# An RWKV kernel with a dense SiLU block: r and k transposed in two row groups behind the previous unit's A product, one ring of five PSUM banks, two units reordered

## Chip, cores, metric

One core of one Trainium2 chip. Times are microseconds (us) of device time for the whole program, medians over several executions. TensorE is the matmul engine, VectorE, ScalarE and GpSimd the three others; PSUM is the matmul output memory in eight banks, SBUF the working memory.

## The reference

```python
# r, k, v: (B=4, H=8, S=768, D=48); w, u: (H, D)
for t in range(S):
    cur = einsum('bhd,bhe->bhde', u[None] * kt, vt)
    y[:, :, t] = einsum('bhd,bhde->bhe', rt, state + cur)
    state = w[None, :, :, None] * state + einsum('bhd,bhe->bhde', kt, vt)
x = y.transpose(0, 2, 1, 3).reshape(B * S, H * D)      # 3072 x 384
h = x @ w_in                                           # 384 -> 2048
return (h * sigmoid(h)) @ w_out                        # 2048 -> 384
```

The kernel cuts time into six chunks of 128 tokens. A *unit* is one chunk of one batch entry: 24 units, unit i = (chunk i // 4, batch i % 4). Inside a unit the recurrence becomes matmuls: r and k are turned (tokens to columns) and multiplied by powers of w; A = kT x rT is masked; y = A x v + r x state; the unit's sum of k x v updates the state.

## The kernel before

The parts that the change touches (cuts marked with `# ...`):

```python
def p1(i, tag="tA", mid=None, spins=0):        # turn r and k, apply the decays
    tr = ps.tile([128, NP, C], FP, name="tr", tag=tag, bufs=3)
    tk = ps.tile([128, NP, C], FP, name="tk", tag=tag, bufs=3)
    spin(spins, tr)                            # keep-warm matmuls
    for t, src in ((tr, rin), (tk, kin)):
        flat = src[n].rearrange("p h d -> p (h d)")
        for p in range(NP):                    # NP = 4 pairs of heads
            nc.tensor.transpose(t[0:PR, p, :], flat[:, 128 * p:128 * p + PR], ident)
    L["rT"] = wrk.tile([PR, NP, C], FP, name="rT")
    nc.vector.tensor_tensor(out=L["rT"], in0=tr[0:PR], in1=lamR, op=ALU.mult)
    # ... kT the same from tk and lamK; if i >= B: ScalarE converts rT to rT16

def p2(i, spins=0):                            # the A product, even and odd heads
    ae = ps.tile([128, NP, C], FP, name="ae", tag="tA", bufs=3)
    ao = ps.tile([128, NP, C], FP, name="ao", tag="tA", bufs=3)
    for p in range(NP):
        nc.tensor.matmul(ae[:, p, :], L["kT"][0:D, p, :], L["rT"][0:D, p, :], ...)
        nc.tensor.matmul(ao[:, p, :], L["kT"][64:PR, p, :], L["rT"][64:PR, p, :], ...)
    # ... VectorE: am = a * maskM for both

for i in range(B + 2, NU):                     # units 6 to 23
    p2(i)
    fill(2)                                    # pieces of the dense block ("fillers")
    bonus_sum(i); bonus_vu(i)
    if i + 1 < NU: front(i + 1)                # p1, v16, ku, rku_f, kc of the next unit
    if i >= NIN: load(i + NIN)
    fill(1)
    p3y(i); p3e(i)                             # y = ..., y16 = y + vu
    if sc < NCH - 1: sums(i); state(i)
    fill(2)
    p4(i)                                      # turn y16
    fill(3)
    # ... refill the list of fillers with the chunk's dense products
```

`hps` is the first dense product (ScalarE takes it to `gT` through SiLU), `ops` the second; `win` and `wout` are their weights. Other names: `am` is A after its mask, `sps` the unit's sum of k x v, `st` and `stb` the state and its 16-bit copy, `xT` the turned y. GpSimd makes `kc`, the decayed k that the sum needs, and `rku_f`, the product of r, u and k; VectorE adds its rows up ("row sum", `bonus_sum`), and v times that is `vu`. Keep-warm matmuls (`spin`) multiply junk, only so that TensorE is busy. PSUM: a ring of 3 banks (tag tA), one of 2 (tag y), one of 3 (tag moe, dense).

## Time and profile before

| | before |
|---|---|
| median of the first runs | 220.91 us (220.13 to 222.15) |
| TensorE busy, of a span of 218.3 us | 205.8 us, 94% |
| saturated stage | 58 to 190 us, TensorE idle 0.2 us |
| transposes of one unit, start to start | 0.87 us |

In lines of the profile, PE is TensorE, PEld its weight loads, DVE VectorE, ACT ScalarE and POOL GpSimd; `out<-in` are tiles, L218 is a line of the kernel, x4 a count. The page's row of slices cuts the span into 40 equal parts and gives TensorE's busy share in tenths; the clock row gives the granted TensorE clock the same way:

```profile
PE   7999588878999999999999999999999999999993
PEclk9999999999999999999999999999999999999999
```

Apart from the first and the last slice, TensorE has gaps in slices 5 to 10 (22 to 55 us) only. This profiled execution had the full clock throughout.

### The profile page before, as it was taken

How to read it: one execution, taken by the hardware profiler on the slowest of the kernel's cores; microseconds unless marked ns; L12 is line 12 of the kernel's file. 1: busy time of each engine (PE TensorE's matmuls, PEld its weight loads, DVE VectorE, ACT ScalarE, POOL GpSimd, SP SyncE). 2: the span in 40 equal slices, each digit the busy share in tenths (PEclk: the TensorE clock that was granted, in tenths of full speed). 3: DMA queues.
4: the chain of work that ended last, by engine and by line, in shares of the span. 5: the costliest groups of instructions: out<-in, count | busy, mean ns of one | idle time of the engine just before them, and what ended most of it. 6: DMA issues, size and time to landing. Idle time of an engine off the chain costs nothing.

```text
span 218.3 us, 4606 instructions
## 1 busy us (share of the span) xinstructions
PE 205.8 (94%) x1778; PEld 137.1 (63%) x1778; DVE 115.0 (53%) x234; ACT 105.4 (48%) x240; POOL 113.1 (52%) x143
## 2 busy tenths in 40 slices
PE   7999588878999999999999999999999999999993
PEld 2776365557777787676567676567676557654561
DVE  6578626745384573685375476366467337420121
ACT  2487876666710563214873124782025771049400
POOL 3399774565835953848664675373475165200000
PEclk9999999999999999999999999999999999999999
DMA  4998999999534750738513465510201000110011
GB/s 95 222 223 154 199 213 188 197 212 183 114 76 104 179 114 3 159 97 175 114 36 75 110 147 116 100 39 0 75 36 38 3 0 16 60 72 0 3 72 72
DMA packets 81662, 22.32 MB, mean 102 GB/s; under 512 B 75368, under 2 KB 81256, under 8 KB 81640
## 3 DMA queue, kind: packets, MB, share of 16 engines
q1 hardware_dynamic: 78360, 18.88, 40.1%
q0 software_dynamic: 3280, 3.15, 8.7%
q8 instruction: 14, 0.23, 0.4%
q14 instruction: 8, 0.07, 0.1%
HBM read 20.45 MB, written 4.72 MB: 115 GB/s over the span
## 4 chain that ended last, share of the span: by engine, by line
PE 84%; ACT 6%; DVE 6%; issue 1%; POOL 1%; DVEq 0%; ACTq 0%
PE ops L329 29%; PE hps L317 24%; PE ae L235 11%; PE tr L218 5%; PE tk L218 3%; PE spin L123 2%; DVE rT L220 2%; PE yT L305 2%; ACT vu L206 2%; PE sps L273 2%; PE y L257 2%; ACT gT L320 1%; PE y L254 1%; PE tr L123 1%; DVE kT L224 1%; DVE am L242 1%
## 5 line engine op out<-in xcount | busy, mean ns | idle before, releaser
L317 PE MATMUL hps<-xT,win 128*128 128x512 f16 (+1 forms) x348 | 70.6, 342 | 1.6 <-ACT gT L320 0.9
L329 PE MATMUL ops<-wout,gT 128*128 128x384 f16 x384 | 69.9, 326 | 0.0
L320 ACT ACTIVATE gT<-hps 128x512 f16<-128x512 f32 (+1 forms) x116 | 58.5, 524 | 20.2 <-PE hps L317 18.2
L329 PEld LDWEIGHTS <-gT 128*128 128x128 f16 x384 | 35.8, 98 | 21.3
L198 POOL TENSOR_TENSOR vu<-vin,rku 128x384 f32<-128x384 f32 x20 | 16.6, 829 | 61.3 <-DVE rku L192 60.1
L317 PEld LDWEIGHTS <-win 128*128 128x128 f16 x348 | 32.1, 98 | 24.2 <-issue 2.6
L242 DVE TENSOR_TENSOR am<-ae,maskM 128x512 f16<-128x512 f32 x24 | 16.6, 691 | 46.1 <-PE ao L237 46.1
L227 ACT CAST rT<-rT 112x512 f16<-112x512 f32 x20 | 12.4, 618 | 50.7 <-DVE rT L220 50.7
L333 DVE COPY osb<-ops 128x384 f32<-128x384 f32 x24 | 13.3, 556 | 33.2 <-PE ops L329 32.7
L235 PEld LDWEIGHTS ae<-rT,kT 48*128 48x128 f32 x192 | 23.1, 187 | 9.1 <-issue 6.7
L235 PE MATMUL ae<-rT,kT 48*128 48x128 f32 x192 | 27.7, 285 | 0.5 <-DVE kT L224 0.2
L237 PE MATMUL ao<-rT,kT 48*128 48x128 f32 x192 | 27.7, 285 | 0.0
L175 POOL TENSOR_TENSOR ku<-kin,u_bc 128x384 f32<-128x384 f32 x24 | 24.1, 1006 | 6.4 <-ACT u_bc L145 6.4
L181 POOL TENSOR_TENSOR rku_f<-rin,ku 128x384 f32<-128x384 f32 x24 | 24.1, 1003 | 1.8
L186 POOL TENSOR_TENSOR kc<-kin,lamC 128x384 f16<-128x384 f32 x24 | 24.0, 999 | 0.0
L237 PEld LDWEIGHTS ao<-rT,kT 48*128 48x128 f32 x192 | 23.1, 187 | 0.0
L220 DVE TENSOR_TENSOR rT<-tr,pi 112x512 f32<-112x512 f32 x24 | 16.6, 690 | 10.4 <-PE tr L218 10.3
L306 ACT COPY xT<-yT 128x384 f16<-128x384 f16 x24 | 11.4, 474 | 17.0 <-PE yT L305 17.0
L242 DVE TENSOR_TENSOR am<-ao,maskM 128x512 f16<-128x512 f32 x24 | 16.3, 681 | 0.0
L224 DVE TENSOR_TENSOR kT<-tk,pi 112x512 f32<-112x512 f32 x24 | 16.3, 681 | 0.0
L291 POOL TENSOR_TENSOR sdec<-st,pi 112x384 f32<-112x384 f32 x16 | 13.3, 834 | 5.2 <-DVE st L287 5.2
L264 DVE TENSOR_TENSOR y<-y,vu 128x384 f16<-128x384 f32 x24 | 13.3, 553 | 4.0 <-PE y L257 2.7
(62 smaller groups left out, 213.9 us busy)
## 6 DMA issues: line engine op xcount, KB each, us to landing
rin<-in_r_dram SPq DMA_DIRECT2D x24, 192.0 KB, 3.4
kin<-in_k_dram SPq DMA_DIRECT2D x24, 192.0 KB, 3.4
vin<-in_v_dram SPq DMA_DIRECT2D x24, 192.0 KB, 3.5
out_dram<-osb SPq DMA_DIRECT2D x24, 192.0 KB, 1.9
wout<-in_moe_w_out_dram POOLq DMA_DIRECT2D x2, 768.0 KB, 10.6
win<-in_moe_w_in_dram POOLq DMA_DIRECT2D x2, 384.0 KB, 7.1
win<-in_moe_w_in_dram POOLq DMA_DIRECT2D x1, 768.0 KB, 11.6
wrow<-in_w_dram SPq DMA_DIRECT2D x1, 1.5 KB
```

Source lines behind the costliest of these rows:

```text
L175: nc.gpsimd.tensor_tensor(out=L["ku"], in0=kin[i % NIN][:, :, 0:D], in1=u_bc, op=ALU.mult)
L181: nc.gpsimd.tensor_tensor(out=L["rku_f"], in0=rin[i % NIN][:, :, 0:D], in1=L["ku"], op=ALU.mult)
L186: nc.gpsimd.tensor_tensor(out=kc[i % NKC][:, :, 0:D], in0=kin[n][:, :, 0:D], in1=lamC, op=ALU.mult)
L218: nc.tensor.transpose(t[0:PR, p, :], flat[:, 128 * p:128 * p + PR], ident)
L220: nc.vector.tensor_tensor(out=L["rT"], in0=tr[0:PR], in1=lamR, op=ALU.mult)
L224: nc.vector.tensor_tensor(out=L["kT"], in0=tk[0:PR], in1=lamK, op=ALU.mult)
L235: nc.tensor.matmul(ae[:, p, :], L["kT"][0:D, p, :], L["rT"][0:D, p, :], start=True, stop=True)
L237: nc.tensor.matmul(ao[:, p, :], L["kT"][64:PR, p, :], L["rT"][64:PR, p, :], start=True, stop=True)
L242: nc.vector.tensor_tensor(out=am, in0=a, in1=maskM.unsqueeze(1).broadcast_to([128, NP, C]), op=ALU.mult)
L317: nc.tensor.matmul(hps, win[:, q, ft * 128:(ft + 1) * 128], xts[sc][:, q, b0:b1, :].rearrange("p b t -> p (b t)"), start=(q == 0), stop=(q ...
L320: nc.scalar.activation(out=gts[sc][:, ft, b0 * C:b1 * C], in_=hps, func=AF.Silu)
L329: nc.tensor.matmul(ops, gts[sc][:, ft, b * C:(b + 1) * C], wout[:, ft, :], start=(ft == 0), stop=(ft == NFT - 1))
```

## The change

Its intent: fewer TensorE cycles for the f32 transposes. Those of 128 tokens by 128 columns become pairs of 64 tokens on the lower and upper half of the array's rows. They stand right behind the A product, which uses row halves too, so that they need no change of tiling mode of their own. That needs four banks at a time, hence one ring of five. Units 4 and 5 are put in a new order, with the conversion of r to 16 bit and the loading of wout later, and the state of chunk 0 read by VectorE alone.

```diff
+    def p1t(i):
+        xs = [ps.tile([128, 2, NP, 64], FP, name="xs", tag="t", bufs=5) for _ in range(2)]
+        for a, src in enumerate((rin, kin)):
+            flat = src[n].rearrange("p h d -> p (h d)")
+            for p in range(NP):
+                for g in range(2):
+                    t = slice(64 * g, 64 * g + 64)
+                    nc.tensor.transpose(xs[g][0:PR, a, p, :],
+                                        flat[t, 128 * p:128 * p + PR], ident[t, t])
+        rk = wrk.tile([PR, 2, NP, C], FP, name="rk")        # rT = rk[:, 0], kT = rk[:, 1]
+    def p1d(i):
+        for g in range(2):
+            nc.vector.tensor_tensor(out=rk[:, :, :, 64 * g:64 * g + 64], in0=xs[g][0:PR],
+                                    in1=lam(g), op=ALU.mult)
+    def r16(i): ...                                         # the 16-bit r, now on its own
-    def p2(i, spins=0):
+    def p2(i, spins=0, nxt=None):
         # ... A product; tiles now tag="t", bufs=5
+        if nxt is not None: p1t(nxt)
         # ... masks
+        if nxt is not None: p1d(nxt)
     # state, chunk 0:
-                nc.scalar.copy(out=st16[b][...], in_=sps[...])
                 nc.vector.tensor_copy(out=dst, in_=sps[p0:p0 + D, :, c0:c0 + D])
+        else:
+            nc.scalar.copy(out=st16[b], in_=st[b])
     # head:
-        p1(s, tag="moe", ..., spins=4 if s else 0)
+        p1(s, ..., spins=2 if s else 0)
-        p2(s, spins=3)
+        p2(s, spins=2)
     # ... units 4 and 5 in a new order; wout issued behind state(a), a = 4
     for i in range(B + 2, NU):
-        p2(i)
-        fill(2)
         bonus_sum(i)
         bonus_vu(i)
+        p2(i, nxt=i + 1 if i + 1 < NU else None)
+        fill(2)
         if i + 1 < NU:
             front(i + 1)                                    # no longer contains p1
+            r16(i + 1)
```

More of the change, by code (lines that the diff above doesn't have):

```diff
@@ L104 @@
     nc.gpsimd.tensor_copy(out=ident16, in_=ident)
-    pi = cst.tile([PR, 2 * NP, C + 1], FP)
+    NT = NP * (C + 1)
+    pif = cst.tile([PR, 2 * NT + 2], FP)
+    pi = pif[:, 0:2 * NT].rearrange("q (a c) -> q a c", c=C + 1)
     nc.gpsimd.memset(pi[:, :, 0:1], 1.0)
@@ L118, in spin @@
         if t is None:
-            t = ps.tile([128, 512], FP, name="spin", tag="y", bufs=2)
+            t = ps.tile([128, 512], FP, name="spin", tag="t", bufs=5)
         else:
@@ L125, in to_cols @@
     def to_cols(row):
-        t = ps.tile([128, 512], FP, name="cols", tag="y", bufs=2)
+        t = ps.tile([128, 512], FP, name="cols", tag="t", bufs=5)
         nc.tensor.transpose(t[0:PR, 0:NP], row.rearrange("p j d -> p (j d)")[:, 0:PR],
@@ L139, in to_rows @@
     def to_rows(dst, cols):
-        t = ps.tile([128, NP, 2, 64], FP, name="rows", tag="y", bufs=2)
+        t = ps.tile([128, NP, 2, 64], FP, name="rows", tag="t", bufs=5)
         for p in range(NP):
@@ L158, with lam @@
     wCT = pi[:, 0:NP, C]
+    def lam(g):
+        t = pif.rearrange("q (a n) -> q a n", a=2)[:, :, 0:NT]
+        return t.rearrange("q a (p c) -> q a p c", c=C + 1)[:, :, :, 64 * g:64 * g + 64]
     lamCT = cst.tile([PR, NP, C], FP)
@@ L207, in bonus_act, with p1 @@
                                  func=AF.Copy, scale=L["rku"][:, h:h + 1])
-    def p1(i, tag="tA", mid=None, spins=0):
+    def p1(i, mid=None, spins=0):
         n = i % NIN
         L = live.setdefault(i, {})
-        tr = ps.tile([128, NP, C], FP, name="tr", tag=tag, bufs=3)
-        tk = ps.tile([128, NP, C], FP, name="tk", tag=tag, bufs=3)
+        tr = ps.tile([128, NP, C], FP, name="tr", tag="t", bufs=5)
+        tk = ps.tile([128, NP, C], FP, name="tk", tag="t", bufs=5)
         spin(spins, tr)
@@ L218, in p1 @@
                 nc.tensor.transpose(t[0:PR, p, :], flat[:, 128 * p:128 * p + PR], ident)
-        L["rT"] = wrk.tile([PR, NP, C], FP, name="rT")
+        rk = wrk.tile([PR, 2, NP, C], FP, name="rk")
+        L["rT"] = rk[:, 0]
         nc.vector.tensor_tensor(out=L["rT"], in0=tr[0:PR], in1=lamR, op=ALU.mult)
@@ L222, in p1, with r16 @@
             mid()
-        L["kT"] = wrk.tile([PR, NP, C], FP, name="kT")
+        L["kT"] = rk[:, 1]
         nc.vector.tensor_tensor(out=L["kT"], in0=tk[0:PR], in1=lamK, op=ALU.mult)
-        if i >= B:
-            L["rT16"] = wrk.tile([PR, NP, C], F16, name="rT16")
-            nc.scalar.copy(out=L["rT16"], in_=L["rT"])
-    def p2(i, spins=0):
-        L = live[i]
-        ae = ps.tile([128, NP, C], FP, name="ae", tag="tA", bufs=3)
-        ao = ps.tile([128, NP, C], FP, name="ao", tag="tA", bufs=3)
+    def p1t(i):
+        n = i % NIN
+        L = live.setdefault(i, {})
+        xs = [ps.tile([128, 2, NP, 64], FP, name="xs", tag="t", bufs=5) for _ in range(2)]
[6 more added lines that the diff above has]
+                                        flat[t, 128 * p:128 * p + PR], ident[t, t])
+        rk = wrk.tile([PR, 2, NP, C], FP, name="rk")
+        L["rT"] = rk[:, 0]
+        L["kT"] = rk[:, 1]
+        L["xs"] = xs, rk
+    def p1d(i):
+        L = live[i]
+        xs, rk = L["xs"]
+        for g in range(2):
+            nc.vector.tensor_tensor(out=rk[:, :, :, 64 * g:64 * g + 64], in0=xs[g][0:PR],
+                                    in1=lam(g), op=ALU.mult)
+    def r16(i):
+        L = live[i]
+        L["rT16"] = wrk.tile([PR, NP, C], F16, name="rT16")
+        nc.scalar.copy(out=L["rT16"], in_=L["rT"])
+    def p2(i, spins=0, nxt=None):
+        L = live[i]
+        ae = ps.tile([128, NP, C], FP, name="ae", tag="t", bufs=5)
+        ao = ps.tile([128, NP, C], FP, name="ao", tag="t", bufs=5)
         spin(spins, ae)
@@ L238, in p2 @@
                              start=True, stop=True)
+        if nxt is not None:
+            p1t(nxt)
         L["am"] = []
@@ L245, in p2 @@
             L["am"].append(am)
+        if nxt is not None:
+            p1d(nxt)
     def p3y(i):
@@ L250, in p3y @@
         v16 = L["v16"]
-        L["y"] = y = ps.tile([128, H, D], FP, name="y", tag="y", bufs=2)
+        L["y"] = y = ps.tile([128, H, D], FP, name="y", tag="t", bufs=5)
         for p in range(NP):
@@ L268, in sums @@
         L = live[i]
-        L["sps"] = sps = ps.tile([128, NP, PW], FP, name="sps", tag="y", bufs=2)
+        L["sps"] = sps = ps.tile([128, NP, PW], FP, name="sps", tag="t", bufs=5)
         kf = kc[i % NKC].rearrange("p h d -> p (h d)")
@@ L284, in state @@
             else:
-                nc.scalar.copy(out=st16[b][p0:p0 + D, :, c0:c0 + D],
-                               in_=sps[p0:p0 + D, :, c0:c0 + D])
                 nc.vector.tensor_copy(out=dst, in_=sps[p0:p0 + D, :, c0:c0 + D])
@@ L301, in p4 @@
             xts[sc] = wrk.tile([128, NQ, B, C], F16, name="xT", bufs=3)
-        yT = ps.tile([128, NQ, C], F16, name="yT", tag="y", bufs=2)
+        yT = ps.tile([128, NQ, C], F16, name="yT", tag="t", bufs=5)
         yf = L["y16"].rearrange("p h d -> p (h d)")
@@ L363, in clear @@
         nc.scalar.copy(out=st[b], in_=zero)
-        nc.scalar.copy(out=st16[b], in_=zero)
     for s in range(B):
-        p1(s, tag="moe", mid=to_cols_u if s == 0 else None, spins=4 if s else 0)
+        p1(s, mid=to_cols_u if s == 0 else None, spins=2 if s else 0)
         nat_v(s)
@@ L403 @@
     bonus_vu(a)
-    nat_ku(b_)
-    for g in range(2):
-        nc.gpsimd.dma_start(
-            out=wout[:, 8 * g:8 * g + 8, :],
-            in_=moe_w_out[1024 * g:1024 * g + 1024, :].rearrange("(f p) n -> p f n", p=128))
-    nat_rk(b_)
     for ft in range(4):
@@ L416, in front @@
     def front(i):
-        p1(i)
         nat_v(i)
@@ L424 @@
     fillers.extend(l1s(0)[4:])
-    p1(a)
+    p1t(a)
+    p1d(a)
     fill(1)
-    nat_v(a)
     sums(0)
     state(0)
+    nat_v(a)
+    r16(a)
+    nat_kc(a)
     fill(1)
-    p2(a)
+    p2(a, nxt=b_)
     fill(1)
+    nat_ku(b_)
+    nat_rk(b_)
+    p3y(a)
+    p3e(a)
     sums(1)
@@ L435 @@
     fill(1)
-    p3y(a)
-    p3e(a)
-    nat_kc(a)
+    sums(a)
+    state(a)
+    for g in range(2):
+        nc.gpsimd.dma_start(
+            out=wout[:, 8 * g:8 * g + 8, :],
+            in_=moe_w_out[1024 * g:1024 * g + 1024, :].rearrange("(f p) n -> p f n", p=128))
+    p4(a)
+    fill(2)
+    r16(b_)
+    nat_v(b_)
+    for i in range(4):
+        load(NIN + i)
+    bonus_sum(b_)
+    bonus_vu(b_)
+    p2(b_, nxt=b_ + 1)
+    nat_kc(b_)
+    fill(2)
     sums(2)
     state(2)
-    fill(1)
-    sums(3)
-    state(3)
-    p1(b_)
-    fill(1)
-    p4(a)
-    sums(a)
-    state(a)
-    fill(1)
-    p2(b_)
-    bonus_sum(b_)
-    bonus_vu(b_)
-    nat_kc(b_)
-    fill(2)
-    nat_v(b_)
-    fill(1)
     p3y(b_)
@@ L460 @@
     state(b_)
-    for i in range(NIN):
-        load(NIN + i)
-    fill(2)
+    load(NIN + 4)
+    load(NIN + 5)
+    fill(1)
     p4(b_)
@@ L467 @@
     front(B + 2)
+    r16(B + 2)
+    sums(3)
+    state(3)
     fill(2)
@@ L470 @@
         sc, b = unit(i)
-        p2(i)
-        fill(2)
         bonus_sum(i)
         bonus_vu(i)
+        p2(i, nxt=i + 1 if i + 1 < NU else None)
+        fill(2)
         if i + 1 < NU:
             front(i + 1)
+            r16(i + 1)
         if i >= NIN:
```

## The prediction

> **What bounds the kernel now.** I read the busy times first, then the windows by stage, then the chain of waits, then single groups of instructions, then the order of time inside one unit. A unit is 128 tokens of one batch entry; there are 24 of them, numbered 0 to 23.
>
> The page and the windows (span, then busy time of TensorE, its weight loads, VectorE, ScalarE, GpSimd, clock, DMA share):
>
> ```profile
> PE 205.8 (94%) x1778; PEld 137.1 (63%) x1778; DVE 115.0 (53%) x234; ACT 105.4 (48%) x240; POOL 113.1 (52%) x143
> ...
> 0.00:30.00 30.00, 25.09 (x211) 16.73 (x212) 19.22 (x51) 19.88 (x63) 21.28 (x35) 1.00 0.98 181
> 30.00:51.00 21.00, 17.51 (x159) 11.57 (x157) 12.08 (x25) 13.90 (x33) 12.11 (x16) 1.00 1.14 196
> 51.00:58.00 7.00, 6.83 (x81) 5.99 (x79) 4.21 (x8) 4.96 (x15) 4.64 (x6) 1.00 0.97 192
> 58.00:190.00 132.00, 131.83 (x1190) 89.58 (x1188) 75.27 (x143) 56.64 (x115) 74.28 (x89) 1.00 0.34 78
> ```
>
> There are three regimes. From 58 to 190 us TensorE never stops (131.83 of 132 us) while no other engine passes 57%; there every microsecond of TensorE work removed shortens the run. From 30 to 51 us (units 4 and 5 and the states of chunk 0) TensorE is idle for 3.5 us, and it waits for VectorE, GpSimd and ScalarE in turn. Before 30 us the four first units form a chain of latencies. After 190 us only the last chunk's two dense products are left.
>
> The transposes as a group, and one unit in order of time (start, duration, engine, line):
>
> ```profile
> L218 PE MATMUL tr<-ident,rin 128*112 128x128 f32 x96 | 14.9, 279 | 0.0
> L218 PE MATMUL tk<-ident,kin 128*112 128x128 f32 x96 | 14.6, 275 | 0.0
> ...
> 70.03 0.60 PE L218 MATMUL tr<-ident,rin 128*112 128x128 f32 x4
> 70.47 0.60 PE L218 MATMUL tk<-ident,kin 128*112 128x128 f32 x4
> 70.90 0.81 PE L329 MATMUL ops<-wout,gT 128*128 128x384 f16 x4
> ```
>
> The mean of 275 ns contains latency. What one costs is the distance of starts: 70.03 to 70.90 us is 0.87 us for eight transposes, 109 ns each, with no idle. The A product of the same unit:
>
> ```profile
> 67.62 0.37 PE L235 MATMUL ae<-rT,kT 48*128 48x128 f32 x1
> 67.63 0.37 PE L237 MATMUL ao<-rT,kT 48*128 48x128 f32 x1
> 67.84 0.27 PE L235 MATMUL ae<-rT,kT 48*128 48x128 f32 x1
> 67.84 0.27 PE L237 MATMUL ao<-rT,kT 48*128 48x128 f32 x1
> 67.95 0.27 PE L235 MATMUL ae<-rT,kT 48*128 48x128 f32 x1
> ...
> 68.51 0.27 PE L237 MATMUL ao<-rT,kT 48*128 48x128 f32 x1
> 68.72 0.50 PE L329 MATMUL ops<-wout,gT 128*128 128x384 f16 x2
> ```
>
> Even and odd heads sit on rows 0 to 47 and 64 to 111; the two products start 0.01 us apart and the next pair follows after 0.11 us. So two row groups really run side by side, weight loads included. The first step is 0.21 us, not 0.11, and so is the step back to full height (68.51 to 68.72): changing between row groups and full array costs about 0.1 us on each side.
>
> **What the Trainium skill says.** "TensorE: Matmul & The Clock Gate", Part 3 on row and column tiling: matmuls in different row groups run concurrently, a few ns apart; the trace agrees (0.01 us). "TensorEngine Tiling (Array Packing)", Key Properties: changing the tiling mode drains the engine; the trace agrees (the two 0.1 us above). The same page, Gotcha 1: different row tiles may not write one PSUM bank at the same time; the change gives each row group its own bank, and no run yet shows what else would happen. "TensorE: Matmul & The Clock Gate", Back-to-back issue gap: N/2.4 GHz plus 2.5 ns. For N=384 that is 162.5 ns and the trace has 0.65 us for four ops matmuls, so 162; for the f32 transposes of 128 columns the measured 109 fits two cycles a column (107 + 2.5).
>
> **The change part by part.**
>
> 1. *Transposes in two row groups.* For 20 units (4 to 23; units 0 to 3 keep the old form) eight transposes of 128 columns become sixteen of 64 columns, in pairs on rows 0 to 63 and 64 to 127. Moving data: 64 columns at two cycles are 53 + 2.5 = 56 ns a pair if the pair is concurrent. Weight load: still 112 columns. Its latency row shows 137 ns for the transposes, 130 for the f16 load of 112 columns, 187 for the f32 load of 128 columns in the A product; the A product's load is hidden in a 110 ns period, so I estimate the transposes' load at some 50 ns net, hidden behind 56. Eight pairs: 0.45 us instead of 0.87, a saving of **0.42 us a unit**. They stand right behind the A product of the unit before, which is in row groups already, so no extra change of mode. 17 units in the saturated stage: 17 x 0.42 = **7.1 us**. The three in the stage laid out anew: 1.3 us, less 0.3 us because unit 4's stand alone and pay both mode changes: **1.0 us**.
>
> 2. *VectorE.* It still multiplies two tiles of 112x512 per unit (690 ns each), only cut by token half over r and k instead of by r and k. No gain and no loss. But the four reads (two masks, two decays) now follow each other: A end + 0.15, then 4 x 0.65 = 2.6 us until the y addition can run, and one output copy (0.56) may push in. TensorE meanwhile does 0.45 (transposes) + 3 fillers of 0.65 + 0.4 (y) + 0.2 (sums) + 2 fillers of 0.65 = 4.3 us before it needs that y. VectorE needs about 0.15 + 2.6 + 0.56 + 0.55 = 3.9 us. Slack 0.4 us: no wait expected. The row sum of unit i moves ahead of its A product, into time in which VectorE waited anyway.
>
> 3. *One ring of five banks instead of 3 + 2.* Per unit seven tiles go through five banks. At the A product four are taken (two A, two transposed); their predecessors (y, sums, y turned) have been read by then. Zero in the saturated stage. In the first four units the transposes no longer borrow the dense product's three banks, so five banks do what eight did; I count at most five tiles alive and expect no wait of size.
>
> 4. *Units 4 and 5 anew.* The state of chunk 0 today is read in four alternating steps by ScalarE and VectorE from one bank; the waits show it:
>
> ```profile
> DVE st L287 <- ACT stb L285: 3.5, 7, 1.2
> ...
> PE sps L273 <- DVE st L287: 1.3, 2, 0.7
> ...
> PE sps L273 <- POOL kc L186: 0.7, 1, 0.7
> PE hps L317 <- ACT gT L320: 0.6, 1, 0.6
> ```
>
>    After the change VectorE reads both halves in a row (0.7 us instead of 1.45) and ScalarE converts from SBUF. I followed the new order by hand with the durations above. TensorE then waits about 0.3 us before y of unit 4, 0.3 before its turning back, and **1.2 us** for GpSimd's kc of unit 5 (which comes behind the two wout issues, 0.9 us each, and vu). That is some 1.8 us where the old order loses about 4 us (3.5 in the window, a little more at its ends): **2.2 us**.
>
> 5. *Head.* Two keep-warm matmuls fewer before the transposes of units 1 to 3, at 0.216 us each; they lay between A and the next transposes, where VectorE idled 0.55, 0.12 and 0.29 us before rT. The gain is the lesser of 0.43 and that idle time each: 0.43 + 0.12 + 0.29 = **0.8 us**. Four ScalarE copies (0.5 us each) go too, but ScalarE waited there.
>
> Sum: 7.1 + 1.0 + 2.2 + 0.8 = 11.1 us off 220.9: about **210 us**. Dense products, output copies and the 20.8 us tail stay as they are.
>
> **The rivals.**
>
> *The pair doesn't run at 56 ns.* If the weight loads of f32 data bound it (112 columns at two cycles would be 93 ns, some 96 a pair), eight pairs cost 0.77 us and the change gives 2 us instead of 8: 216 us. If the two groups ran one after the other it gives nothing: 218. For: none of the rows shows a 64-column transpose. Against: the A product's loads overlap across the groups, and the load rows (137 against 187) say one cycle a column.
>
> *A new wait takes its place.* VectorE's in-order queue (mask, mask, decay, decay, output copy, y) or the row sum at the head of the loop, which waits for GpSimd's rku_f and holds back the masks. In the saturated stage GpSimd has 5.2 us of work per 7.6 us unit, so it keeps up; at unit 6, right after the new layout, it may be a microsecond late. If the y addition came 0.3 us late in every unit, 18 x 0.3 = 5.4 us would be lost: 215 us.
>
> *The late wout.* Its issue moves from 28.6 us to about 40 us, behind unit 4's state; its landing took 8.4 to 12.8 us, when DMA ran at its full 200 GB/s. It is first read at 58.2 us now and at about 54 us then. If input loads delay it, TensorE stands still for one to three us: 211 to 213 us.
>
> *The clock.* Fewer keep-warm matmuls might let the granted clock fall in the head; the gaps there are about a microsecond, the clock row is at full speed throughout, so I give this little.
>
> **Range and chances.** The 7 us of the saturated stage are the firm part, if the pairs are concurrent; the 4 us of layout and head are good to about 2 us either way. That puts 8 in 10 cases between 207 and 214 us. Faster by over 2% means below 216.5 us; it needs only half of the sum. 0.91 faster, 0.07 within 2%, 0.02 slower.
>
> **What would show it.** In the changed kernel: sixteen transposes with 64 columns, a pair every 56 ns and 0.45 us from the last A pair to the next filler's mode step; a saturated stage with TensorE over 99% and units 0.42 us shorter; waits of sums for kc of about 1 us near 42 us; first ops matmul near 54 us without a wait for DMA; states in chunk 0 without the VectorE-ScalarE alternation. The prediction is wrong if a pair takes 90 to 110 ns, if TensorE waits for y (VectorE) in every unit, or if it stands before the first ops.

## The result

The changed kernel is correct and took **210.78 us** (210.09 to 210.90, four runs) against 220.52 us for the kernel before in the same comparison. The ratio is 0.954, with a 95% interval of 0.948 to 0.960; on the chip of the first experiments it was 0.953 (0.951 to 0.954; 210.51 against 221.00 us).

The page and the windows of the changed kernel, with columns as in the prediction (the last figures are the clock, the DMA share and GB/s):

```profile
PE 197.5 (94%) x1928; PEld 129.0 (62%) x1928; DVE 115.2 (55%) x234; ACT 101.9 (49%) x232; POOL 113.7 (54%) x143
...
PEclk9999669999999999999999999999999999999999
...
0.00:30.00 30.00, 25.08 (x199) 16.21 (x200) 19.06 (x51) 18.47 (x58) 18.98 (x32) 0.89 0.97 180
30.00:54.00 24.00, 21.20 (x257) 14.82 (x256) 16.49 (x34) 16.66 (x39) 19.63 (x24) 1.00 1.10 185
54.00:182.00 128.00, 127.86 (x1350) 85.62 (x1348) 76.41 (x144) 56.73 (x120) 75.04 (x88) 1.00 0.39 88
```

TensorE's busy time fell by 8.3 us. The saturated stage is still saturated (127.86 of 128 us). The four A products of the head, from the first to the last start, took 11.41 us instead of 12.44, but unit 4's A product came at 32.41 us, as before (32.37). In between the clock was at half, from 22.7 to 29.6 us, so that it is 0.89 over the first 30 us. That fault was not in the profile of before. The longest pause of TensorE in the microseconds ahead of it (start, duration, and in brackets the idle time before and what ended it):

```profile
22.54 0.35 PE L344 MATMUL yT<-ident,y 128*128 128x128 f16 x3 [1.39 <-DVE y L303]
```

The transposes of the same kind of unit, in order of time (start and duration in us), with the step of the A product ahead and the first filler behind, and their group:

```profile
71.44 0.27 PE L272 MATMUL ao<-rk 48*128 48x128 f32 x1
71.55 0.39 PE L245 MATMUL xs<-ident,rin 64*112 64x64 f32 x8
71.78 0.39 PE L245 MATMUL xs<-ident,kin 64*112 64x64 f32 x8
72.10 0.82 PE L368 MATMUL ops<-wout,gT 128*128 128x384 f16 x4
...
L245 PE MATMUL xs<-ident,rin 64*112 64x64 f32 x160 | 7.9, 216 | 0.0
```

Sixteen transposes take from 71.55 to about 72.00 us, and the step back to full height (0.1 us, which the A product paid before) now comes behind them. Four pairs go from 71.55 to 71.78, 57 ns each. Units in the stage of ops are 7.62 us apart, from A product to A product, instead of 8.04.

What TensorE and VectorE wait for from 30 to 60 us in the changed kernel (total, times, longest):

```profile
PE sps L312 <- POOL kc L194: 1.3, 1, 1.3
PE hps L356 <- ACT gT L359: 1.1, 1, 1.1
...
DVE rku L200 <- POOL rku_f L189: 3.0, 2, 2.6
```

The first is the wait that the prediction named. The second is new; the account of it, tested in e7 below, is this: at unit 6 VectorE's queue stands at the row sum, which waits for GpSimd; masks and decays behind it come late, ScalarE's conversion of r comes late, and gT behind that.

### The profile page after: what moved, and what is told of

Read it like the earlier page. It is cut to its first block, busy times and chain, and to the rows that moved or that the text cites. A ratio compares the mean times of both kernels' runs of the same rounds, so it can differ in the third digit from the quotient of the medians.

```text
span 209.2 us, 4922 instructions
## 1 busy us (share of the span) xinstructions
PE 197.5 (94%) x1928; PEld 129.0 (62%) x1928; DVE 115.2 (55%) x234; ACT 101.9 (49%) x232; POOL 113.7 (54%) x143
## 4 chain that ended last, share of the span: by engine, by line
PE 80%; DVE 3%; POOL 3%; ACT 1%; issue 1%; ACTq 0%
PE ops L368 30%; PE hps L356 29%; PE ae L270 9%; PE xs L245 4%; PE y L296 2%; PE sps L312 2%; PE yT L344 2%; PE y L293 1%; DVE am L279 1%; POOL wout L477 1%; DVE rk L256 1%; POOL sdec L330 1%; ACT gT L359 1%; PE ao L272 1%; POOL kc L194 0%
## 5 line engine op out<-in xcount | busy, mean ns | idle before, releaser
L356 PE MATMUL hps<-xT,win 128*128 128x512 f16 (+1 forms) x348 | 71.6, 350 | 1.9 <-ACT gT L359 1.1
L368 PE MATMUL ops<-wout,gT 128*128 128x384 f16 x384 | 68.2, 326 | 0.0
L270 PEld LDWEIGHTS ae<-rk 48*128 48x128 f32 x192 | 23.1, 187 | 9.9 <-issue 6.2
L256 DVE TENSOR_TENSOR rk<-xs,pif 112x512 f32<-112x512 f32 x40 | 25.6, 681 | 5.6 <-PE xs L245 5.6
L270 PE MATMUL ae<-rk 48*128 48x128 f32 x192 | 27.7, 285 | 0.9 <-DVE rk L233 0.9
L272 PE MATMUL ao<-rk 48*128 48x128 f32 x192 | 27.7, 285 | 0.0
L326 POOL CAST stb<-st 112x384 f16<-112x384 f32 x16 | 8.1, 504 | 34.7 <-DVE st L321 34.0
L262 ACT CAST rT<-rk 112x512 f16<-112x512 f32 x20 | 12.4, 620 | 22.5 <-DVE rk L256 22.5
L272 PEld LDWEIGHTS ao<-rk 48*128 48x128 f32 x192 | 23.1, 187 | 0.0
L330 POOL TENSOR_TENSOR sdec<-st,pif 112x384 f32<-112x384 f32 x16 | 13.4, 836 | 7.2 <-DVE st L324 7.2
```

Source lines behind the costliest of these rows:

```text
L256: nc.vector.tensor_tensor(out=rk[:, :, :, 64 * g:64 * g + 64], in0=xs[g][0:PR], in1=lam(g), op=ALU.mult)
L330: nc.gpsimd.tensor_tensor(out=sdec[b], in0=st[b], in1=wCT.unsqueeze(2).broadcast_to([PR, NP, PW]), op=ALU.mult)
L356: nc.tensor.matmul(hps, win[:, q, ft * 128:(ft + 1) * 128], xts[sc][:, q, b0:b1, :].rearrange("p b t -> p (b t)"), start=(q == 0), stop=(q ...
L368: nc.tensor.matmul(ops, gts[sc][:, ft, b * C:(b + 1) * C], wout[:, ft, :], start=(ft == 0), stop=(ft == NFT - 1))
```

## The experiments

All twelve kernels gave correct results. The mean granted clock of the executions is listed, since 3.4 us at half clock lowers it by 0.008 (3.4 x 0.5 of some 209). The calls ran on three chips: the changed kernel again and e1 to e3 on one, e4 to e7 on a second, e8 to e11 on a third. Medians of different calls are compared below as they are; where a difference is small, the ratios to before, with their intervals, decide.

| kernel | median us | ratio to before | mean clock of its executions |
|---|---|---|---|
| before (call 1; calls 2 and 3) | 221.0; 220.97 and 221.0 | | 0.988 to 0.992; 0.981 to 1.0 |
| changed, again | 210.51 | 0.953 (0.951 to 0.954) | 0.984 to 0.991 |
| e1_spins | 211.38 | 0.956 (0.955 to 0.958) | 0.992 |
| e2_full_height | 216.94 | 0.981 (0.978 to 0.984) | 0.991 to 0.998 |
| e3_group_after_group | 214.56 | 0.972 (0.970 to 0.975) | 0.984 to 0.992 |
| e4_old_place | 224.03 | 1.015 (1.012 to 1.019) | 0.985 to 0.992 |
| e5_two_rings | 229.34 | 1.038 (1.034 to 1.043) | 0.985 to 0.992 |
| e6_kc_first | 209.95 | 0.951 (0.948 to 0.954) | 0.98 to 0.992 |
| e7_sum_behind_masks | 209.04 | 0.947 (0.944 to 0.950) | 0.982 to 0.992 |
| e8_old_place_late_r16 | 217.60 | 0.984 (0.981 to 0.986) | 0.984 to 0.992 |
| e9_both | 207.86 | 0.941 (0.939 to 0.944) | 0.983 to 0.992 |
| e10_both_warm | 206.74 | 0.936 (0.933 to 0.938) | 0.998 to 1.0 |
| e11_old_state | 210.58 | 0.952 (0.949 to 0.956) | 0.984 to 0.998 |

### The changed kernel again

> The changed kernel once more, unchanged, so that the experiments of this call have it on their own chip. All theories: 209.5 to 211.5 us. The trace of the changed kernel had the granted clock at half from 22.9 to 29.7 us; if that depends on chance, some executions will show a mean clock near 1.0 and be 1.5 to 2 us shorter; if it belongs to the kernel, all will show 0.98 to 0.99.

All four executions had a clock of 0.984 to 0.991; so the drop is no accident of one profile. But the seven executions of the kernel before on the same chip had 0.988 to 0.992 as well. With the later calls, before ran at 1.0 in 219.87 to 220.13 us, at 0.992 in 220.94 to 221.12 us and at 0.981 to 0.983 in 222.09 to 222.25 us. A window of 3.4 us at half clock costs about 1 us, and both kernels usually lose one. Where the kernel before loses it was not profiled; e4 and e8 below, which have its head, were at half from 38 to 41 us, between units 4 and 5. At like clock the change gains some 10.5 us.

### e1_spins: the keep-warm matmuls of the head restored

> Undoes one part: 4 and 3 keep-warm matmuls in the head again, instead of 2 and 2. Theory A (the fewer keep-warm matmuls let the clock fall): clock 1.0, the 24 half-wide hps matmuls at 26 us take 2.9 us instead of 4.7, and the time falls by 1.0 to 2.0 us against the changed kernel, less up to 0.8 us for the longer head. Theory B (the pause of TensorE from 21 to 24.5 us, while it waits for y and the masks, lets it fall; the keep-warm matmuls before 20 us are too early to matter): clock 0.98 to 0.99 again, time equal or up to 0.8 us longer.

```diff
-        p1(s, mid=to_cols_u if s == 0 else None, spins=2 if s else 0)
+        p1(s, mid=to_cols_u if s == 0 else None, spins=4 if s else 0)
-        p2(s, spins=2)
+        p2(s, spins=3)
```

0.87 us longer than the changed kernel, with the clock at 0.992 in all four executions. Theory A is out: these matmuls do not prevent the drop. And taking them out was worth about 0.9 us. Theory B's reason holds only in part: the pause behind the A product of unit 3 shrank from 1.39 us to 0.22, and the drop came all the same, at 26.8 us, behind a later pause:

```profile
22.61 0.34 PE L344 MATMUL yT<-ident,y 128*128 128x128 f16 x3 [0.22 <-DVE y L303]
...
25.79 1.82 PE L356 MATMUL hps<-xT,win 128*128 128x256 f16 x12 [1.18 <-ACT xT L345]
```

### e2_full_height: everything but the row groups

> Everything of the change but the row groups: the transposes of the next unit stand behind the A product, but as eight of full height and 128 columns. Theory (a concurrent pair takes 56 ns): 20 units lose 0.42 us each, 8.4 us, less 0.3 us for unit 4: 218 to 219.5 us, so layout, ring and head are worth some 2 us against before. Rival (the gain came from the new layout and order, the row groups only moved along): 211 to 213 us.

```diff
-                for g in range(2):
-                    t = slice(64 * g, 64 * g + 64)
-                    nc.tensor.transpose(xs[g][0:PR, a, p, :], flat[t, ...], ident[t, t])
+                nc.tensor.transpose(xs[a] ..., flat[:, 128 * p:128 * p + PR], ident)
     # p1d then multiplies xs[0] by lamR and xs[1] by lamK
```

Theory expected 218 to 219.5 us, 7.5 to 9.0 over the changed kernel; it is 6.4, below that range. The rival's 0.5 to 2.5 us are out. In order of time, from the last step of A to the filler:

```profile
71.08 0.27 PE L272 MATMUL ao<-rk 48*128 48x128 f32 x1
71.28 0.65 PE L244 MATMUL xs<-ident,rin 128*112 128x128 f32 x4
71.76 0.60 PE L244 MATMUL xs<-ident,kin 128*112 128x128 f32 x4
72.20 0.81 PE L368 MATMUL ops<-wout,gT 128*128 128x384 f16 x4
```

From the end of A (71.19 us, one step of 0.11 behind its last start) to the filler are 1.01 us; in the changed kernel 0.55 (71.55 to 72.10). The distance between units' A products says the same: 8.08 against 7.62 us. From unit 7 to unit 23 that is 129.03 against 121.69 us, so the row groups are worth 7.3 us there. But the kernel without them reached unit 7's A product at 54.01 us against 55.00: up to there they gave nothing. That stage waits for other engines, and unit 6, with its wait for gT, even took 8.95 us without them and 9.60 with them. ScalarE's conversion of r in that unit, first with the row groups (the changed kernel again), then without:

```profile
50.70 0.62 ACT L262 CAST rT<-rk 112x512 f16<-112x512 f32 x1 [1.36 <-DVE rk L256]
```

```profile
49.72 0.62 ACT L262 CAST rT<-rk 112x512 f16<-112x512 f32 x1 [0.24 <-DVE rk L256]
```

VectorE's two multiplications began at 49.34 and 49.00 us and took 1.28 us. Cut by tokens, the conversion of r starts behind the second of them; cut by r and k, behind the first, 0.69 us long. So the row groups have a cost of their own here, which e4 shows again. TensorE's wait for gT behind it was 1.1 us with them and 0.3 us without.

### e3_group_after_group: one row group after the other

> The same sixteen transposes of 64 columns in two row groups, but all eight of the first group and then all eight of the second. Theory (the gain is the two groups running side by side): each takes 56 ns alone, 0.90 us a unit instead of 0.45; 20 x 0.45 = 9 us longer, 219 to 220.5 us. Rival (the gain is that 64 columns at half height are cheaper in themselves, or TensorE overlaps the groups over a distance of eight instructions): 211 to 212.5 us.

```diff
-        for a, src in enumerate((rin, kin)):
-            for p in range(NP):
-                for g in range(2):
+        for g in range(2):
+            for a, src in enumerate((rin, kin)):
+                for p in range(NP):
```

4.1 us longer, between the two expectations. One unit in order of time (the program has r x4 and k x4 of the lower group, then r x4 and k x4 of the upper):

```profile
63.47 0.39 PE L245 MATMUL xs<-ident,rin 64*112 64x64 f32 x4
63.69 0.22 PE L245 MATMUL xs<-ident,kin 64*112 64x64 f32 x1
63.70 0.27 PE L245 MATMUL xs<-ident,rin 64*112 64x64 f32 x1
63.75 0.27 PE L245 MATMUL xs<-ident,kin 64*112 64x64 f32 x2
...
63.97 0.38 PE L245 MATMUL xs<-ident,kin 64*112 64x64 f32 x4
64.29 0.34 PE L368 MATMUL ops<-wout,gT 128*128 128x384 f16 x1
```

The upper group's first r starts 0.01 us after the lower group's first k and ahead of its second. So, by the start times of the trace, TensorE runs a matmul of a free row group ahead of some that stand before it in the program; r and k are interleaved like this in all 20 units. Part of the two groups overlaps: 0.72 us (63.47 to 64.29, less the 0.1 us of the mode step) instead of the 0.90 of no overlap and the 0.45 of pairs. The 0.27 us more than in pairs are also the difference of the units, 7.90 against 7.62 us, and 16 of them are 4.3 us. Half height with this partial overlap gives 0.18 us of a unit against e2 (8.08 to 7.90); the alternating order gives the rest.

### e4_old_place: the row groups alone, at the old place

> The row groups alone: the kernel before, with the transposes of units 4 to 23 as sixteen of 64 columns in two row groups, but at their old place between two fillers; layout, rings and head as before. Theory (a pair takes 56 ns, but here each unit pays a change of tiling mode of its own, 0.1 us before, 0.1 in the first step, 0.1 after): 0.45 + 0.3 instead of 0.87 us, 0.1 to 0.15 us a unit, 2 to 2.5 us in all: 218.5 to 219 us. Rival (the place does not matter): 17 saturated units save 0.38 us or more each, 214 to 214.7 us.

```diff
     # in the kernel before, p1 of units 4 to 23 is replaced by p1t: row groups, both
     # multiplications, then the conversion of r, all at p1's place
+        xs = [ps.tile([128, 2, NP, 64], FP, name="xs", tag="tA", bufs=3) for _ in range(2)]
```

3.1 us **slower than before** (1.2 to 1.9%); neither theory nor rival had that. In the stage of ops it does what the theory says: 7.87 instead of 8.04 us a unit. The units of hps became longer: the two with half-wide hps (6 and 9) took 9.2 instead of 8.41 us. TensorE's waits from 60 to 190 us, and ScalarE's conversion in one such unit:

```profile
PE hps L345 <- ACT gT L348: 3.3, 7, 1.1
...
81.41 1.29 DVE L252 TENSOR_TENSOR rk<-xs,pif 112x512 f32<-112x512 f32 x2 [0.33 <-PE xs L246]
...
82.78 0.62 ACT L255 CAST rT<-rk 112x512 f16<-112x512 f32 x1 [1.65 <-DVE rk L252]
```

Before, the conversion needed one multiplication (r). Cut by tokens, it needs both, 1.3 us, and ScalarE's queue stands still before it for 1.65 us with the SiLU of the next hps behind.

### e8_old_place_late_r16: the same with the conversion moved back

> The old-place kernel was 3 us slower than before, although its ops units are 0.18 us shorter (7.87 against 8.05). Here it gets one part more of the change: ScalarE converts r to 16 bit later, behind the next two fillers (in the first two units behind the fill ahead of their y). Theory (in the old place both halves of r and k must have been multiplied before the conversion can run, it blocks ScalarE's queue, gT comes late and the hps matmuls wait, 3.3 us between 60 and 190 us): those waits go, 218 to 220 us. Rival (the loss is in the mode changes or in the rings): 223 to 224.5 us again.

```diff
         fill(2)
+        if i + 1 < NU:
+            r16(i + 1)            # was inside the front of unit i + 1
         p4(i)
```

6.4 us faster than at the old place with the early conversion, 3.4 us faster than before; the waits for gT from 60 to 190 us are gone altogether. The theory holds, though the time lies 0.4 us below its range: the loss came from the conversion's place in ScalarE's queue. At the old place the row groups give 0.17 us an ops unit, behind the A product 0.42. Units 6 and 9, at 8.41 us before, are 7.90 here; that is more than 0.17, so the later conversion would probably have helped the kernel before too. No run shows that.

### e5_two_rings: no common ring

> Undoes the one ring: A product and turned tiles in a ring of 3 banks, all else in one of 2, the first units' transposes in the dense product's 3 banks, as before; everything else as in the changed kernel. Theory (the second turned tile needs a fourth bank while both A tiles are unread): TensorE waits in each unit behind the A product until the first mask has been read, about 0.85 us from the end of the A product; 17 to 20 units, 14 to 17 us longer than the changed kernel: 224 to 228 us. Rival (the ring is only tidier): 210 to 211.5 us.

```diff
-   tag="t", bufs=5               # all the small PSUM tiles
+   tag="tA", bufs=3              # ae, ao, xs
+   tag="y", bufs=2               # y, sps, yT, spin, cols, rows
+   tag="moe", bufs=3             # tr, tk of the first four units
```

18.8 us longer than the changed kernel, more than the theory's 14 to 17. TensorE's wait is the one expected:

```profile
PE xs L245 <- DVE am L279: 15.0, 19, 2.0
```

Units are 8.60 us apart. With three banks the upper group's tile waits for the first mask. With the banks split in this way the new place costs more than it gives; other splits were not tried.

### e6_kc_first and e7_sum_behind_masks: the two waits that are left

> One suspected wait taken away: GpSimd issues the two wout transfers behind vu and kc of unit 5 instead of ahead of them (1.8 us of GpSimd). Theory: the wait of sums for kc at 43 us (1.27 us in the changed kernel) goes, and 0.5 to 1.2 us of it reaches the end: 209.3 to 210.0 us; the wout transfers land some 2 us later, still before the first ops matmul. Rival (GpSimd is the busy engine of this stage, so that the time comes back as a longer wait for unit 6's masks and for gT): 210.3 to 210.8 us, with the hps wait for gT grown from 1.1 to about 2 us.

```diff
-    for g in range(2): nc.gpsimd.dma_start(out=wout[...], ...)      # behind state(a)
     # ...
     nat_kc(b_)
+    for g in range(2): nc.gpsimd.dma_start(out=wout[...], ...)
```

0.56 us shorter, inside the theory's range, but on another chip and with intervals that overlap (0.948 to 0.954 against 0.951 to 0.954). The traces agree with it: from unit 4's A product to unit 7's are 22.30 us instead of 22.87. The wait for kc is gone; unit 6 came to its A product 0.78 us sooner, counted from unit 4's, but took 9.81 instead of 9.60 us. So the rival is right for a part: the rest came back in front of gT, whose wait stayed at 1.1 us.

> At unit 6 alone the row sum (which VectorE waits 2.6 us to begin, for GpSimd's rku_f) goes behind the masks and decays in VectorE's queue, as it stood in the kernel before. Theory (the late row sum holds back masks and decays, so ScalarE converts r of unit 7 late and the hps matmuls wait 1.1 us for gT): masks start near 47 instead of 48.4 us, the wait for gT at 52 us goes, 0.8 to 1.2 us shorter: 209.3 to 209.7 us. Rival (ScalarE has too much to do there anyway, 256-column silu at 0.33 us each against 0.33 us of matmul plus its three copies): wait halves at most, 0 to 0.5 us shorter.

```diff
-        bonus_sum(i); bonus_vu(i)
+        if i > B + 2: bonus_sum(i); bonus_vu(i)
         p2(i, nxt=i + 1 if i + 1 < NU else None)
+        if i == B + 2: bonus_sum(i); bonus_vu(i)
```

1.47 us shorter, more than expected: unit 6 took 8.15 instead of 9.60 us, and the wait for gT is gone. So the changed order of the row sum was bad for this unit; whether it helps in units 7 to 23 no run shows.

### e9_both and e10_both_warm

> The changed kernel with both mends: wout issued behind kc of unit 5, and unit 6's row sum behind its masks. Alone they gave 0.6 and 1.5 us against 210.5. Theory (two waits one after the other, 1.3 us for kc and 1.1 us for gT): they add up, 208.0 to 208.6 us. Rival (GpSimd is busy all through this stage, the second mend has already taken what the first can give): 208.9 to 209.3 us.

Both edits at once: 2.65 us shorter than the changed kernel, somewhat more than the sum of the two (2.03) and 0.14 us below the theory's range. They stand one after the other in time and add up. TensorE waits for neither kc nor gT.

> As e9_both, with eight more keep-warm matmuls in the pause of TensorE between the A product of unit 3 and the first hps matmuls (six behind the A product, two behind the first turned y), where it waits anyway. Theory (it is this pause that halves the clock for one or two windows of 3.4 us, and the hps matmuls at half clock cost about 1 us): mean clock 1.0 in all executions, 0.7 to 1.2 us shorter than e9_both. Rival (those hps matmuls wait for win or for xT anyway, so the slow clock is hidden): clock 1.0 and the same time within 0.3 us.

```diff
         p2(s, spins=2)
+        if s == B - 1: spin(6, warm)        # behind the A product of unit 3
         if s > 1: p4(s - 2)
     # behind the loop
+    spin(2, warm)
```

1.12 us shorter still, **206.74 us**, and the mean clock 0.998 to 1.0 in all five executions. The windows of the two kernels, e9_both first (TensorE busy comes first, the clock third from the end):

```profile
22.00:24.00 2.00, 0.54 (x4) 0.27 (x4) 2.00 (x4) 2.00 (x10) 1.92 (x3) 1.00 1.13 180
24.00:26.00 2.00, 1.64 (x15) 1.26 (x16) 1.67 (x4) 1.59 (x6) 2.00 (x3) 0.64 1.20 196
26.00:28.00 2.00, 2.00 (x12) 1.40 (x11) 0.00 (x0) 1.23 (x4) 0.67 (x1) 0.51 1.12 202
```

```profile
22.00:24.00 2.00, 1.71 (x11) 0.57 (x9) 2.00 (x5) 2.00 (x11) 1.92 (x3) 1.00 1.21 200
24.00:26.00 2.00, 1.76 (x20) 1.43 (x21) 1.54 (x4) 1.90 (x7) 2.00 (x3) 1.00 1.18 195
26.00:28.00 2.00, 1.33 (x14) 1.10 (x13) 0.00 (x0) 1.42 (x5) 0.55 (x1) 1.00 1.13 204
```

The keep-warm matmuls fill 22 to 24 us, where TensorE was busy for 0.54 of 2 us, and the half clock behind it does not come. So theory holds and the rival falls: work in these pauses keeps the clock, and the drop costs about 1.1 us. This version beats both kernels.

Is it one long pause that counts? The stretches at half clock in the traces last 3.41 us or twice that, so I cut each of the fourteen traces into windows of 3.41 us, from the first rise of its clock. Twelve have a drop, and in the window just before it TensorE was busy for 40 to 60%. No busier window was followed by one (up to 190 us, ahead of the tail). Five windows of 52 to 60% (one each in before, e4, e5, e6 and e8) were not either, so this is no sharp threshold. In e10 the lowest window has 76%. The share of busy time goes with the drop better than the length of a single pause.

### e11_old_state: the state of chunk 0 read by two engines again

> Undoes one part of the changed kernel: in chunk 0 the state is again read from PSUM by ScalarE and VectorE in turn, two halves each, and the 16-bit states are cleared in the head as before. Theory (VectorE's and GpSimd's queue are on the chain from 36 to 43 us, so the four alternations of some 0.7 us count in part): 0.7 to 1.8 us longer than the changed kernel, 211.2 to 212.3 us. Rival (they lie beside the waits for kc and gT): 210.3 to 210.9 us.

```diff
-                nc.vector.tensor_copy(out=dst, in_=sps[p0:p0 + D, :, c0:c0 + D])
-        else:
-            nc.scalar.copy(out=st16[b], in_=st[b])
+                nc.scalar.copy(out=st16[b][...], in_=sps[p0:p0 + D, :, c0:c0 + D])
+                nc.vector.tensor_copy(out=dst, in_=sps[p0:p0 + D, :, c0:c0 + D])
```

210.58 us against 210.51: no difference. The alternation is back, but beside the longer waits: the wait for kc grew from 1.3 to 1.6 us, and unit 6 took 9.53 instead of 9.60. The rival holds; this part of the change was worth nothing measurable in this order (the six executions spread over 2 us).

## Why the prediction was right

The time, 210.78 us for 210.0, lies in the range, and the two large terms came out near their size. At like clock the change gains 10.5 us (221.00 to 210.51) where the prediction's sum was 11.1.

1. *The transposes in row groups* (0.42 us a unit, 7.1 us in the saturated stage): shown. A pair takes 57 ns, eight pairs 0.45 us, and units are 7.62 instead of 8.04 us apart. From unit 7's A product to unit 23's, all of that stage but its ends, are 16 such units and not 17: 6.7 us. Directly, that stretch fell from 127.83 to 121.68 us with one filler (0.65 us) more in it: 6.8 us at equal work. The slower-pair rival (96 ns) is out; so is "one group after the other", and e3 shows that the order in the program decides how much they overlap.
2. *The 1.0 us for the three transposes before that stage*: this step failed. In e2 the kernel without row groups was no later at unit 7. I had taken matmul time as path time in a stage that I had described as waiting for other engines, and had counted the token cut of the multiplications as "no gain and no loss": at unit 6 it held ScalarE's conversion back (e2).
3. *VectorE in the saturated stage* (no wait, slack 0.4 us): right; that stage has TensorE busy for 127.86 of 128 us.
4. *The ring* (zero wait): right, and e5 shows what it avoids.
5. *Units 4 and 5* (2.2 us): the wait for kc was foreseen at 1.2 us near 42 us and measured at 1.27 us at 43 us. But the argument led with the state's alternation, and e11 shows that it gave nothing measurable. The rival "row sum at unit 6 a microsecond late" came true, as 2.6 us of VectorE and 1.1 us of TensorE; its cost belonged in the sum. e7 puts it at 1.5 us.
6. *Head* (0.8 us): e1 measures 0.87. It restores one keep-warm matmul ahead of each A product too, which the prediction's term left out, so the close fit is in part luck.
7. *The clock* ("I give this little"): the reason given, that the clock row is at full speed throughout, was true of one profile and false of most executions. It changed the comparison little only because the kernel before usually loses a window too.
8. *wout late*: no wait was seen, but the first ops matmul began at 57.5 us, not 54. The transfers were issued at 39.4 and 40.3 us and the slower one took 13.9 us, so it can have landed as late as 54.2: had TensorE been on the predicted time, wout would have come only just in time.

Head, layout and the rest together: 10.5 less 6.7 is 3.8 us, where the prediction had 4.0 (1.0 + 2.2 + 0.8); e2, which has all of it but the row groups, is 4.1 us faster than before. Of these, 0.9 us is the keep-warm matmuls (e1). The remaining 2.9 us belong to the new order of units 4 and 5 and the later conversion of r together; no run here takes these apart, except for the state (nothing measurable). That the sum fits so well is partly luck: 1.0 us that was not there and 1.5 us that was not counted stand against gains that I had under-counted, and which of them is not shown.

## What to carry to other kernels

Half-height f32 transposes paid most where the two halves alternate in the program and stand where the array is in row groups already (0.46 us a unit against e2; 0.18 without alternation, 0.17 at the old place); plan the PSUM banks for that place first. When an operation is cut along another axis, look at who reads its parts: here the 16-bit conversion suddenly needed both, and an in-order queue turned a faster TensorE into a slower kernel. Where TensorE pauses for a microsecond or two, look at the clock in several executions and not in one profile.

## What the Trainium skill lacked or had wrong

- "TensorE: Matmul & The Clock Gate", Part 3, says that matmuls start and end in program order, "strict FIFO, no reordering". In e3_group_after_group a matmul of the upper row group started at 63.70 us, ahead of lower-group matmuls (63.75 us and later) that stand before it in the program.
- The same page, in the table of "Why this matters for your kernels", warns of pauses of TensorE of over some 3 us. In the changed kernel the clock fell to half at 22.7 us although the longest pause before it was 1.39 us (21.1 to 22.5 us); eight keep-warm matmuls of some 0.22 us prevented it (e10_both_warm, clock 0.998 to 1.0). The page's section "A second HAM failure mode" does tell of short idles between groups of matmuls that make the clock swing, but without a number; here the windows before the drops were 40 to 60% busy. That it stays at half for one or two windows of 3.4 us agrees with the page's Part 1 (3.41 and 6.83 us in the traces).
- No page gives the cost of f32 transposes (the same page, Part 4, has durations for bf16 ones only) or of the change of tiling mode ("TensorEngine Tiling (Array Packing)" says only that it drains). Here: 109 ns for one of 128 columns at full height, 57 ns for a pair of 64 columns in two row groups, and about 0.1 us for each of three steps (before, within and after) when a group of matmuls in row halves stands between full-height ones.
